# Batch 0's score pieces regrouped: the first three key blocks together by halves of the queries, the later ones in twos

## The chip, the cores and the metric

One core of a Trainium2 chip. The metric is the device time of one execution in microseconds (us), as a median of repeated runs; a profile gives in addition the span of one execution, which here is about 2 us shorter than its time.

## The reference

Grouped attention followed by a feed-forward layer with a squared ReLU, in float32:

```python
# q: 8 x 16 x 384 x 64, k and v: 8 x 4 x 384 x 64 (each kv head serves 4 query heads)
scores = (1 / 8) * q @ k^T ;  attn = softmax(scores) ;  o = attn @ v
x = o as 3072 x 1024
out = (max(x @ w_in, 0) ** 2) @ w_out        # w_in 1024 x 2048, w_out 2048 x 1024
```

## The kernel before

The kernel records all operations with their dependencies and an assumed duration, in a Python loop that at each step chooses what TensorE does next; the recorded order is then fixed for each engine. A *unit* is one block of 128 keys of one kv head, 12 in a batch; its scores have 2 x 768 columns. A *piece* is a part of them that goes through one pair of PSUM banks, `2 * (u % 2)` (u is here the piece's number), and one exponential on ACT:

```python
    def burst_small(b, pieces, base):
        n, c0, wide = (b * NU + pieces[0][0]) % NEX, pieces[0][1], pieces[0][2]
        ...                                     # scores: two matmuls (row halves) per unit in it, L341
        src = ps[:, base:base + 2, 0:total].rearrange("p x (k c) -> p x k c", k=len(pieces))
        dst = expT[:, n:n + len(pieces), :, c0:c0 + wide].rearrange("p k x c -> p x k c")
        R.add("scalar", lambda e: e.activation(dst, src, AF.Exp, scale=0.125), ...)     # L351

    for group in ((0, 1), (2, 3), (4, 5), (6, 7), (8, 9), (10, 11)):
        if 0 < group[0] < NU - 2:
            smalls += [[(u, 0, 512)] for u in group] + [[(u, 512, 256) for u in group]]
        else:
            smalls += [[(u, c0, 384)] for c0 in (0, 384) for u in group]
```

For batch 0 the rest of the head is, on TensorE: transposes of keys (L298) and queries (L315), attention times v in halves of 18 matmuls (L367; a half needs three units of its kv group), transposes of the result (L400), and the first four up-projection tiles (L425, 32 matmuls). Between these stand the transposes that batch 1 needs. The recorder lets the latter in by

```python
        if turn_q and (b == 0 or pairs < 6 or x_done[0] == 8) and (...):     # b: batch of the transpose
```

so after the sixth attention half they wait until all eight are transposed. After the head comes "the stretch": batch 1's scores and the other 12 up-projection tiles of batch 0 in fours (L462). Its first four need the third and fourth of eight blocks of w_in. The loads stand in POOL's queue in a fixed order, here its middle:

```python
    load_w_in(1)
    load_v(1)
    dup_k(1)
    for i in range(2, 6):
        load_w_in(i)
    aug_v(1, "gpsimd")            # waits for v of batch 1
    for i in range(6, 8):
        load_w_in(i)
```

The softmax here doesn't subtract the row's maximum and nothing guards it: scores larger than these inputs give would overflow.

## Time and profile before

| | |
|---|---|
| median, range of 3 runs | 419.39 us, 419.33 to 420.1 |
| span of the profiled execution | 1110.1 us |
| exponentials of batch 0 | 8 of 768 elements, 12 of 1024 |
| w_in, w_out | 8 blocks of 512 KB, 4 of 1024 KB |

The profile shows an execution 2.65 times as long as the timed ones.

### The profile page before, as it was taken

What the parts mean: (1) busy time and instruction counts of PE and PEld (TensorE: products, weight loads), DVE (VectorE), ACT (ScalarE), POOL (GpSimd) and SP (SyncE); (2) the same over time, 40 slices, a digit from 0 to 9 for tenths busy, and PEclk for the clock granted to TensorE, in tenths of its full rate; (3) what the DMA queues carried; (4) which work ended last, traced back from release to release, by engine and by line L of the source; (5) the groups of instructions that cost most, each with busy time, mean ns of one, the idle gap of its engine ahead of it and who ended that gap; (6) DMA issues with size and microseconds to landing.
All of it is one profiled execution on the core that took longest, in us unless ns stands there. A gap on an engine that the chain in (4) does not pass through costs nothing.

```text
span 1110.1 us, 9624 instructions
## 1 busy us (share of the span) xinstructions
PE 1107.0 (100%) x4330; PEld 446.8 (40%) x4330; DVE 203.8 (18%) x434; ACT 169.6 (15%) x181; POOL 48.0 (4%) x63
## 2 busy tenths in 40 slices
PE   9999999999999999999999999999999999999999
PEld 5544523454233532345323363243632336234323
DVE  3312201131011310114001141012300123001100
ACT  5233000330023100230003300032000320001100
POOL 7100101000100010000100000000000000000000
DMA  9950626102600070000700013000110001000000
GB/s 186 203 72 1 99 53 90 15 1 49 106 16 1 9 125 29 10 1 15 119 28 10 1 22 69 29 10 0 24 34 29 1 1 29 29 28 1 0 28 29
DMA packets 96921, 44.40 MB, mean 40 GB/s; under 512 B 77296, under 2 KB 90864, under 8 KB 96880
## 3 DMA queue, kind: packets, MB, share of 16 engines
q0 software_dynamic: 36544, 17.44, 12.2%
q1 hardware_dynamic: 59664, 25.86, 9.6%
q8 instruction: 34, 0.56, 0.2%
q10 hardware_dynamic: 672, 0.49, 0.1%
q14 instruction: 7, 0.06, 0.0%
HBM read 35.65 MB, written 12.58 MB: 43 GB/s over the span
## 4 chain that ended last, share of the span: by engine, by line
PE 100%; DVE 0%; issue 0%
PE ps L524 41%; PE ps L462 35%; PE ps L367 8%; PE ps L341 8%; PE ps L425 6%; PE ps L588 1%; PE ps L315 0%; PE ps L298 0%; PE ps L400 0%; DVE y_sb L533 0%
## 5 line engine op out<-in xcount | busy, mean ns | idle before, releaser
L524 PE MATMUL ps<-w_out_sb,h2T 128*128 128x512 bf16 (+2 forms) x784 | 460.1, 823 | 0.0
L462 PE MATMUL ps<-xT,w_in_sb 64*128 64x384 bf16 x1728 | 415.1, 681 | 0.0
L524 PEld LDWEIGHTS ps<-w_out_sb,h2T 128*128 128x128 bf16 x784 | 135.6, 175 | 309.0 <-issue 308.8
L462 PEld LDWEIGHTS ps<-xT,w_in_sb 64*128 64x128 bf16 x1728 | 153.7, 170 | 232.1 <-issue 221.8
L351 ACT ACTIVATE expT<-ps 128x1024 bf16<-128x1024 f32 (+1 forms) x146 | 146.8, 1012 | 583.7 <-PE ps L341 583.6
L475 DVE TENSOR_SCALAR hr<-ps 128x384 f32<-128x384 f32 x108 | 55.2, 553 | 371.5 <-PE ps L462 371.5
L341 PE MATMUL ps<-qT,kT 64*128 64x256 bf16 (+2 forms) x384 | 114.0, 651 | 0.0
L533 DVE COPY y_sb<-ps 128x512 f32<-128x512 f32 (+2 forms) x49 | 33.4, 681 | 406.5 <-PE ps L524 406.5
L367 PEld LDWEIGHTS ps<-v_aug,expT 128*128 128x128 bf16 x1152 | 87.1, 141 | 16.5 <-issue 12.9
L367 PE MATMUL ps<-v_aug,expT 128*128 128x65 bf16 x1152 | 90.8, 281 | 0.0
L425 PE MATMUL ps<-xT,w_in_sb 128*128 128x384 bf16 x160 | 73.1, 684 | 0.0
L341 PEld LDWEIGHTS ps<-qT,kT 64*128 64x128 bf16 x384 | 29.6, 150 | 54.5 <-issue 33.7
L482 DVE TENSOR_TENSOR h2T<-hr 128x384 bf16<-128x384 f32 x102 | 50.0, 551 | 0.0
L425 PEld LDWEIGHTS ps<-xT,w_in_sb 128*128 128x128 bf16 x160 | 27.4, 173 | 41.1 <-issue 41.0
L382 DVE TENSOR_TENSOR o_sb<-ps,rinv 128x384 bf16<-128x384 f32 x64 | 35.7, 557 | 2.2
L435 ACT ACTIVATE h2T<-hr 128x384 bf16<-128x384 f32 x20 | 10.5, 523 | 137.2 <-DVE hr L433 137.2
L479 ACT ACTIVATE h2T<-hr 128x384 bf16<-128x384 f32 x6 | 3.1, 523 | 158.9 <-DVE hr L475 158.9
L275 POOL COPY v_aug<-v_st 128x768 bf16<-128x768 bf16 x8 | 6.6, 830 | 460.0 <-PE ps L367 415.2
L376 DVE RECIPROCAL rinv<-ps 128x6 f32<-128x6 f32 x64 | 12.4, 194 | 51.1 <-PE ps L367 51.1
L433 DVE TENSOR_SCALAR hr<-ps 128x384 f32<-128x384 f32 x20 | 11.2, 558 | 54.5 <-PE ps L425 54.5
L241 POOL DMA_DIRECT2D q_st<-in_q_dram x17 | 14.8, 881 | 0.9 <-POOLq L829 0.8
L209 POOL DMA_DIRECT2D k_st<-in_k_dram x7 | 5.3, 755 | 156.2 <-DMA qT<-q_st 156.2
(29 smaller groups left out, 79.3 us busy)
## 6 DMA issues: line engine op xcount, KB each, us to landing
out_dram<-y_sb SPq DMA_DIRECT2D x47, 256.0 KB, 2.0
q_st<-in_q_dram POOLq DMA_DIRECT2D x14, 384.0 KB, 7.5
w_in_sb<-in_moe_w_in_dram POOLq DMA_DIRECT2D x8, 512.0 KB, 14.3
w_out_sb<-in_moe_w_out_dram POOLq DMA_DIRECT2D x4, 1024.0 KB, 27.6
v_st<-in_v_dram POOLq DMA_DIRECT2D x8, 192.0 KB, 8.4
k_st<-in_k_dram POOLq DMA_DIRECT2D x7, 192.0 KB, 3.8
q_st<-in_q_dram POOLq DMA_DIRECT2D x3, 192.0 KB, 5.4
xT<-o_sb SPq DMA_TRANSPOSE x28, 2.7
```

The source lines that it names most:

```text
L241: i = R.add("gpsimd", lambda g: g.dma_start(q_st[st][:, h0:h1, :], q[b, h0:h1].rearrange("h (p j) d -> p h (j d)", j=NJ)), writes=[("q_st" ...
L341: mm = pe.matmul(ps[:, base + x, m * wide:(m + 1) * wide], kT[b % 2][64 * x:64 * x + 64, u, :], q_cols(b, u // NJ, x, c0, c0 + wide))
L351: R.add("scalar", lambda e: e.activation(dst, src, AF.Exp, scale=0.125), reads=keys, writes=[("expT", (b * NU + u) % NEX, t) for u, _, _ i ...
L367: m = pe.matmul(po[:, f - 6 * s2, 0:D + 1], w, v_aug[b % 2][:, g * NJ + j, 0:D + 1], start=(j == 0), stop=(j == NJ - 1))
L376: R.add("vector", lambda e: e.reciprocal(rinv[r].ap().unsqueeze(2), po[:, :, D:D + 1]), reads=[("bank", i)], writes=[("rinv", r)], cost=0.22)
L382: R.add("vector", lambda e: e.tensor_tensor(dst, srcv, rbv, ALU.mult), reads=[("bank", i), ("rinv", r)], writes=[("o_sb", o, s2)], cost=0.48)
L425: m = pe.matmul(bank(i)[:, 0:S], w_in_sb[:, kc, c * 128:(c + 1) * 128], xT[b % NXT][:, kc, :], start=(kc == 0), stop=(kc == NKC - 1))
L462: m = pe.matmul(bank(4 + xs[x])[:, 0:S], w_in_sb[r, kc, c * 128:(c + 1) * 128], xT[b % NXT][r, kc, :], start=(phase < 2 and kc == 0), stop ...
L475: R.add("vector", lambda e, r=r, i=i: e.tensor_scalar_max(hr[r][:, :], bank(4 + i)[:, 0:S], 0.0), reads=[("bank", 4 + i)], writes=[("hr", ...
L482: hr_read[r] = (R.add("vector", lambda e, c=c, r=r: e.tensor_tensor(h2T[:, c, :], hr[r][:, :], hr[r][:, :], ALU.mult), reads=[("hr", r)], ...
L524: m = pe.matmul(bank(i)[:, 0:n], h2T[:, c, i3 * 128:(i3 + 1) * 128], w_out_sb[:, c, c0:c1], start=(c == 0), stop=(c == NFC - 1))
L533: R.add("vector", lambda e: e.tensor_copy(ysl, bank(i)[:, 0:n]), reads=[("bank", i)], writes=[("y", yb)], cost=0.08 + n / 960)
```

## The change

Its intent: ACT should have three pieces to do, not two, before it needs the second half of the first queries, and the first kv group should be complete earlier.

```diff
-    for group in ((0, 1), (2, 3), (4, 5), (6, 7), (8, 9), (10, 11)):
-        if 0 < group[0] < NU - 2:
+    for group in ((0, 1, 2), (3, 4), (5, 6), (7, 8), (9, 10), (11,)):
+        if len(group) == 2:
```

## The prediction

> **What bounds the kernel now.** I read the head of the page first, because its span does not fit the times. The medians of the timed runs are 419.39 us (419.33 to 420.1), the profiled execution took 1110.1. Next the chain that ended last in order of time, for the pace of the matmuls:
>
> ```profile
> span 1110.1 us, 9624 instructions
> PE 1107.0 (100%) x4330; PEld 446.8 (40%) x4330; DVE 203.8 (18%) x434; ACT 169.6 (15%) x181; POOL 48.0 (4%) x63
> ...
> 46.53 8.47 PE ps L425 x19
> 55.00 1.24 PE ps L341 x4
> 56.24 5.32 PE ps L462 x24
> ...
> 122.08 54.81 PE ps L524 x92
> 176.88 14.22 PE ps L462 x64
> ```
>
> The columns of the last five are start, length, engine, tile, line and count. 54.81 us for 92 matmuls of 512 columns is 596 ns each, 8.47 us for 19 of 384 columns is 446 ns, both 0.86 columns per ns, though the granted clock is listed as 1.000. So the execution I can look into ran TensorE at a pace that the timed runs can't have had: 2.65 times the time. In it TensorE is busy all the time and everything else hides behind it; the waits of TensorE in the first batch can't be read off it. ACT, DVE and transfer durations should not depend on that, and I use them.
>
> To find the head in the timed runs I rescale. At a full pace of N/2.4 + 2.5 ns (see below) 512 columns are 215.8 ns and 384 are 162.5, so the factors are 596/215.8 = 2.76 and 446/162.5 = 2.74; for 65 columns 76.6 ns (8.27 us for 108 in the chain) against 29.6, 2.59. After 55.00 us, where the scores of the second batch start, the chain holds some 457 us of line 524, 386 of 462, 60 of 425, 77 of 367 and 78 of 341. Rescaled: 166 + 141 + 22 + 30 + 28 = 387 us (estimate). That leaves 419.4 - 387 = 32 to 33 us for the head, with a microsecond or two of tail in it. TensorE's own work in the head is about 50.5 us of the slow trace (4.47 to 55.00), 18.4 us at full pace, and it begins at about 4.5. So TensorE should idle some 9 us in the head of a timed run. The head is what this change touches, and it is bound there by something other than TensorE.
>
> The candidate is the row of exponentials on ACT, with what feeds it:
>
> ```profile
> L351 ACT ACTIVATE expT<-ps 128x1024 bf16<-128x1024 f32 x138 | 140.4, 1024 | 577.5 <-PE ps L341 577.4
> L351 ACT ACTIVATE expT<-ps 128x768 bf16<-128x768 f32 x8 | 6.4, 810 | 6.2 <-PE ps L341 6.2
> ...
> 7.16 1.51 ACT L351 ACTIVATE expT<-ps 128x768 bf16<-128x768 f32 x2 [2.19 <-PE ps L341]
> 8.02 0.36 DVE L322 COPY qT<-ps 128x384 bf16<-128x384 bf16 x1 [1.56 <-PE ps L315]
> 8.31 0.83 POOL L275 COPY v_aug<-v_st 128x768 bf16<-128x768 bf16 x1
> 9.31 0.81 ACT L351 ACTIVATE expT<-ps 128x768 bf16<-128x768 f32 x1 [0.65 <-PE ps L341]
> 10.75 0.81 ACT L351 ACTIVATE expT<-ps 128x768 bf16<-128x768 f32 x1 [0.62 <-PE ps L341]
> ```
>
> In the timeline ACT does two exponentials, then stands for 0.65 us, does one, stands for 0.62. Its second pair needs the second half of the first kv group's queries, which only reaches qT with the DVE copy at 8.02 to 8.38. That is the gap the change aims at. Two exponentials of 768 back to back took 1.51 us, two of 1024 took 1.94 (timeline at 11.79). Batch 0 has 8 of the former and 12 of the latter: 4 x 1.51 + 6 x 1.94 = 17.7 us if never held up. In the slow trace they take 18.55 us within 30.3 (7.16 to 37.5), so ACT waits 11.8 us among them.
>
> **What the skill says.** "TensorE: Matmul & The Clock Gate", section "Back-to-back issue gap": N/2.4 + 2.5 ns warm; this trace shows 596 ns where that gives 215.8, so it does not agree, and I take the formula for the timed runs only because 387 + 32 fits 419. "ScalarE: Activation LUTs", section "What ACT_TABLE_LOAD costs": an ACTIVATE with immediates takes 186 + 0.833 N ns, and neighbours overlap by about 93. That gives 826 ns at 768 and 1039 at 1024; the rows show 810 and 1024, and the pair 1.51 = 2 x 0.81 - 0.11. It agrees.
>
> **The change, part by part.** It changes the list of score pieces of batch 0 alone. Before: units 0 and 1 by halves of 384 queries, units 2 to 9 in pairs as 512, 512, 2 x 256, units 10 and 11 by halves. After: units 0, 1, 2 by halves (six pieces of 384), pairs (3,4), (5,6), (7,8), (9,10), and unit 11 by halves (two). Both are 8 x 768 and 12 x 1024 elements: **ACT work 0, TensorE score columns 0, DVE work 0.** The built orders of instructions agree: SP and POOL are the same, and TensorE differs only up to the first tiles of the stretch in which batch 1 is scored. Three things move.
>
> (a) The third piece becomes (unit 2, first half), which needs no second half of the queries. What this gains is ACT's gap at full pace, not the 0.65 us of the slow trace. By hand: first keys cast at 3.70, transposed and copied (0.36) by about 4.65; first queries cast at 4.20, transposed, copied by about 5.15; scores 0.15 later, 0.35 long; first exponential at about 5.7, second to 7.15. The second half of the queries is cast at 4.97 whatever the pace, its transposes follow the two score pieces at about 5.75, its copy ends near 6.5, just as the first pair of banks comes free, and its scores are there at about 6.9 to 7.0. So at full pace ACT stands for 0 to 0.3 us. Gain 0 to 0.3, taken as 0.15.
>
> (b) Group 0 of the kv heads is complete after six pieces of 384 (4.5 us of ACT) instead of 4 x 0.755 + 3 x 1.02 = 6.1, and its first half after three (2.3, then v_aug at 9.14 us holds it) instead of five (4.0). So TensorE gets attention work 1.5 us earlier, while it is idle anyway, and less piles up later. Counting pieces, the eight attention halves become ready at 3.4, 4.5, 8.6, 10.7, 12.7, 13.7, 17.5, 18.3 us of ACT time against 4.0, 6.1, 8.1, 9.1, 13.2, 15.3, 16.8, 18.3. The first two halves stand as nine and nine matmuls around a score piece (one later half did before), so those scores wait up to 0.3 us less. ACT's room to lose is about 32 - 5.7 - 17.7 - 6 (end work, next) = 2 to 3 us over the head; I guess that a fifth of it goes. Gain 0 to 1.0, taken as 0.5.
>
> (c) The end. The last exponential is followed by the last attention half. Its group's first half becomes ready one piece later than before (17.5 against 16.8). And 12 transposes of batch 1's keys and queries, which stood inside the head (rows of lines 298 and 315 between score pieces), move behind the last transposes of o: 24 stand there now, 12 before. TensorE after the last exponential: before 18 attention matmuls (0.6), 26 up-projections x 0.1625 (4.2), 18 transposes x 0.056 (1.0) = 5.8; after 0.6 + 23 x 0.1625 (3.7) + 30 x 0.056 (1.7) = 6.0. Cost 0.2. DVE has six copies there in place of three to four (0.36 or 0.56 each), beside 17 up-projections (2.8 us), so they are mostly hidden; 0.1 for it.
>
> Sum: -0.15 - 0.5 + 0.2 + 0.1 = -0.35 us. Everything after is the same program, TensorE-bound, and only shifts. 419.39 - 0.35 = about 419.0.
>
> **Rivals.** One: transfers set the pace and swallow any shift. For it: they run at 184 to 207 GB/s in each 5 us window from 5 to 60 us; w_in's last two blocks land at 37.6 and 40.2 us (22.5 + 15.1, 23.3 + 16.9), the w_out blocks at about 45 to 62, the queries of batch 2 at about 65. Against it: in rescaled time the stretch begins near 32, wants those w_in blocks near 43, w_out's second half near 65, and scores of batch 2 stand behind 64 matmuls put there as filler (176.88 above). If it holds: 419.4. Two: the halted ACT is real, the gap is as large as in the slow trace or larger (a cold TensorE in the first microseconds doubles its transposes), and the filled attention takes away most ACT waits: -1.5 us, 417.9. For it: 2 to 3 us are missing in my account of the head. Against it: TensorE is in order, and the transposes of groups 1 and 2 wait for their query transfers (landing at 6.7 and 8.9) in both orders. Three: the end work grows by more than 0.3, because the transposes and their copies now come between the last xT chunk and the second batch, and its first scores also follow 8 quad matmuls: +0.8 us, 420.2.
>
> **Range and chances.** The known spread of three runs is 0.8 us; the parts can err by about 0.7 together. Predicted 419.0 us, range 418.0 to 420.0. Two per cent is 8.4 us, as much as all of TensorE's idle time in the head, and no work is added: faster by over 2% 0.01, within 2% 0.98, slower 0.01.
>
> **What would show it.** In the changed profile: 8 exponentials of 768 and 12 of 1024 in batch 0; ACT's third exponential following the second without a gap; attention matmuls before the first piece of 2 x 256; 24 transposes together ahead of the last 17 up-projections; from there on the same groups and durations. If that profile runs at full pace, the first score of batch 1 should stand at about 32 us, and ACT's waits among the twenty exponentials should sum to 2 or 3. In a slow one again, the span should move by under 1 us, since the sum of TensorE work is the same but for a few warm-up matmuls. The prediction is wrong if the head's end moves by over 1 us either way, if TensorE turns out to wait for w_in or batch 2's queries, or if the pace of TensorE itself differs between the kernels.

## The result, and the profile after

Ratios here and below are the mean time of one kernel's fast runs over that of the other's in the same rounds, so not quite the ratio of the medians quoted.

| | before | changed | ratio, 95% interval |
|---|---|---|---|
| with the prediction | 420.10 (5 runs) | 419.83 (5) | 1.0002, 0.9987 to 1.0017 |
| repeated (a2) | 419.54 (9 runs) | 419.53 (5) | 0.9999, 0.9987 to 1.0012 |

No gain shows. The times alone cannot exclude 0.35 us either, since its ratio, 0.9992, lies in both intervals. That 419.83 lies in the range is no credit to the reasons: no change at all lies in it too. The profiles decide, and in them the reasons given for the gain fail.

The changed kernel's page begins:

```profile
span 418.2 us, 9601 instructions
```

Its timeline on ACT, in the first 30 us (start, length, engine, line, what, count, idle before and its releaser):

```profile
5.79 16.81 ACT L351 ACTIVATE expT<-ps 128x768 bf16<-128x768 f32 x20 [0.76 <-PE ps L341]
```

All twenty exponentials of batch 0 stand without a gap, from 5.79 to 22.60. That looks like success; only the same view of the kernel before at full pace can tell. It is the first experiment.

### The profile page after: what moved, and what is told of

It reads as the page before. It is cut to its first block, busy times and chain, and to the rows that moved or that the text cites. A ratio compares the mean times of both kernels' runs of the same rounds, so it can differ in the third digit from the quotient of the medians.

```text
span 418.2 us, 9601 instructions
## 1 busy us (share of the span) xinstructions
PE 413.4 (99%) x4308; PEld 236.2 (56%) x4331; DVE 198.6 (47%) x434; ACT 159.0 (38%) x181; POOL 48.0 (11%) x63
## 4 chain that ended last, share of the span: by engine, by line
PE 97%; ACT 2%; issue 0%; DVE 0%
PE ps L524 39%; PE ps L462 34%; PE ps L367 8%; PE ps L341 7%; PE ps L425 6%; ACT expT L351 2%; PE ps L588 1%; PE ps L400 0%; PE ps L298 0%; PE ps L315 0%; DVE y_sb L533 0%
## 5 line engine op out<-in xcount | busy, mean ns | idle before, releaser
L524 PE MATMUL ps<-w_out_sb,h2T 128*128 128x512 bf16 (+2 forms) x761 | 165.7, 375 | 1.2
L462 PE MATMUL ps<-xT,w_in_sb 64*128 64x384 bf16 x1728 | 160.3, 323 | 0.0
L524 PEld LDWEIGHTS ps<-w_out_sb,h2T 128*128 128x128 bf16 x784 | 75.2, 98 | 86.6
L462 PEld LDWEIGHTS ps<-xT,w_in_sb 64*128 64x128 bf16 x1728 | 83.1, 94 | 57.8 <-DVE hr L475 2.1
L341 PE MATMUL ps<-qT,kT 64*128 64x512 bf16 (+2 forms) x384 | 54.3, 326 | 0.3 <-ACT expT L351 0.3
L367 PEld LDWEIGHTS ps<-v_aug,expT 128*128 128x128 bf16 x1152 | 37.0, 97 | 5.7 <-issue 1.1
L367 PE MATMUL ps<-v_aug,expT 128*128 128x65 bf16 x1152 | 39.1, 193 | 0.2 <-issue 0.2
L425 PE MATMUL ps<-xT,w_in_sb 128*128 128x384 bf16 x160 | 27.7, 326 | 0.0
L341 PEld LDWEIGHTS ps<-qT,kT 64*128 64x128 bf16 x384 | 17.8, 94 | 15.6 <-issue 2.1
L425 PEld LDWEIGHTS ps<-xT,w_in_sb 128*128 128x128 bf16 x160 | 15.4, 98 | 9.7 <-DVE xT L406 0.2
```

The source lines that it names most:

```text
L341: mm = pe.matmul(ps[:, base + x, m * wide:(m + 1) * wide], kT[b % 2][64 * x:64 * x + 64, u, :], q_cols(b, u // NJ, x, c0, c0 + wide))
L367: m = pe.matmul(po[:, f - 6 * s2, 0:D + 1], w, v_aug[b % 2][:, g * NJ + j, 0:D + 1], start=(j == 0), stop=(j == NJ - 1))
L425: m = pe.matmul(bank(i)[:, 0:S], w_in_sb[:, kc, c * 128:(c + 1) * 128], xT[b % NXT][:, kc, :], start=(kc == 0), stop=(kc == NKC - 1))
L462: m = pe.matmul(bank(4 + xs[x])[:, 0:S], w_in_sb[r, kc, c * 128:(c + 1) * 128], xT[b % NXT][r, kc, :], start=(phase < 2 and kc == 0), stop ...
L524: m = pe.matmul(bank(i)[:, 0:n], h2T[:, c, i3 * 128:(i3 + 1) * 128], w_out_sb[:, c, c0:c1], start=(c == 0), stop=(c == NFC - 1))
```

## The experiments

**a1: the kernel before, unchanged.**

> The kernel before, unchanged, for a profile at full TensorE pace (the first one ran at a third of it) and as a control of the noise. Ratio 1.000 within 0.002. Theory A (the exponentials of batch 0 already stand without a gap at full pace, so the change had nothing to win): the twenty exponentials take 16.8 to 17.3 us from 5.8, as in the changed kernel, and batch 1's first scores stand at 29.3 to 29.8 us. Theory B (the change did win in the head and lost it again): the exponentials here take 17.5 to 19 us, with gaps, and batch 1's first scores stand 0.5 us or more later than the changed kernel's 29.58, or the stretch after them is shorter.

Ratio 1.0002 (0.9987 to 1.0018), and a profile, span 418.2. Its timeline on ACT, then on TensorE further on:

```profile
5.77 16.91 ACT L351 ACTIVATE expT<-ps 128x768 bf16<-128x768 f32 x20
...
28.65 0.60 PE L341 MATMUL ps<-qT,kT 64*128 64x512 bf16 x4
29.09 1.46 PE L462 MATMUL ps<-xT,w_in_sb 64*128 64x384 bf16 x16
...
31.04 0.83 PE L462 MATMUL ps<-xT,w_in_sb 64*128 64x384 bf16 x8 [0.48 <-DMA w_in_sb<-in_moe_w_in_dram]
```

The kernel before has no gap in this row either: 16.91 us against 16.81, and 16.80 in e2 further down, which has the same order. This is theory A; B's 17.5 to 19 us fail. The gaps of 0.65 and 0.62 us in the slow profile came with its slow TensorE. They are absent although in this execution the second half of the queries was cast later (5.17 us) than in the changed kernel's profile (4.52).

My 29.3 to 29.8 us for batch 1's scores missed, because the two orders put them in different places: directly behind the up-projections here, after 8 matmuls of L462 in the changed kernel (29.47 there). The comparable mark is the end of the 32 up-projections, called **the head's end** from here on. (The chain's starts lie 0.07 to 0.17 us behind the timeline's here, so times are compared within one view.) The last line shows something new: TensorE waits for a w_in block, and in this execution the chain of what ended last runs through that transfer.

```profile
15.11 1.47 POOL k_dup L270
16.57 0.81 POOL w_in_sb L252
17.39 13.52 DMA w_in_sb<-in_moe_w_in_dram
```

It also shows why the block is late: in POOL's queue the copy of batch 1's keys (`dup_k(1)`) stands before this load, and here it had to wait for these keys until 15.11 us.

**a2: the changed kernel, unchanged.**

> The changed kernel, unchanged, 5 rounds more on the same chip as the control. Both theories: ratio 0.998 to 1.002; if the prediction's 0.35 us were there, 0.9992. The profile repeats: twenty exponentials from 5.8 to 22.6 without a gap, first scores of batch 1 at about 29.6, a wait of TensorE for w_in of about 0.4 us near 30.7.

Ratio 0.9999. The row and the scores repeat; the wait for w_in does not: in the first profile of this kernel the block landed at 30.66, its weights went in at 30.71, 0.37 us late, and the matmuls lost 0.16; here it landed at 29.83, in time. In a1 it was 30.91; in f1, shown further down, 29.69. So this landing moves by over a microsecond between executions, and it follows the issue: POOL issued the load at 17.39 us in a1, and at 15.66 in f1, where the keys had landed 1.7 us sooner.

From here I had two suspects: the row of exponentials as the bound of the head, with nothing won in it, and the w_in landing as a pin that hides what is won. e1 to e4 take the last of ACT's work away, take the pin away, or both. In e1 to e4 TensorE's order is unchanged to the last instruction.

**e1: ACT's last two exponentials cut short.** They do 16 of 384 queries, and DVE sets the rest to 1.0 at the start. Wrong, though it passed the comparison: with these inputs (0.1 times a normal draw) the exponentials are near 1.

```diff
+        w = 16 if b == 0 and pieces in smalls[-2:] else wide
-        src = ps[:, base:base + 2, 0:total].rearrange(...)
+        src = ps[:, base:base + 2, 0:total].rearrange(...)[:, :, :, 0:w]
-        dst = expT[:, n:n + len(pieces), :, c0:c0 + wide].rearrange(...)
+        dst = expT[:, n:n + len(pieces), :, c0:c0 + w].rearrange(...)
```

> Kernel before, but the last two exponentials of batch 0 do 16 of 384 queries (wrong result on purpose), TensorE's order untouched: ACT's row ends about 1.1 us sooner, near 21.6 us. Theory P (the arrival of w_in's fourth block near 30.8 us pins the stretch, so nothing won in the head is kept): batch 1's first scores move from 28.65 to 27.6-28.0, TensorE's wait for w_in grows from 0.5 to 1.2-1.6 us, total 0.0 to -0.2 us (ratio 0.9995 to 1.000). Rival R (the head's end sets the time, the change merely won nothing there): total -0.7 to -1.1 us (ratio 0.9974 to 0.9983).

Ratio 1.0001 (0.9988 to 1.0015). ACT's timeline, then the chain:

```profile
5.72 15.41 ACT L351 ACTIVATE expT<-ps 128x768 bf16<-128x768 f32 x19 [0.47 <-PE ps L341]
21.59 0.20 ACT L351 ACTIVATE expT<-ps 128x32 bf16<-128x32 f32 x1 [0.46 <-PE ps L341]
...
28.49 0.54 PE ps L341 x4
```

ACT is done at 21.79 in place of 22.68 in a1 and 22.55 in e2, and the head still ends at 28.49; e2, with all exponentials, has 28.60. These 0.11 us are not the cut's: the chains of the two profiles are apart by 0.11 already at the fifth score piece (8.69 and 8.80 us), long before it. So 0.8 to 0.9 us less at the end of ACT's row is worth nothing. The total is what theory P said, but its stage is wrong: the scores come no earlier for the cut, and there is no longer wait for w_in. Both theories assumed that the end of ACT's row bounds the head's end, and that falls: the last short exponential even waits for its scores. What a faster ACT in the whole row would do was not tested.

**e2: the pin loosened.** Batch 1's v load is moved behind w_in's sixth block (and its copy behind the eighth), after the orders were made, so that all compute engines but POOL have the old order.

```diff
+    MOVES = [("v1", "w5"), ("aug1", "w7")]     # operation, and the one it is put behind, before emit()
```

> Kernel before, only batch 1's v load moved behind w_in's sixth block and its copy behind the eighth, so w_in's blocks 3 to 6 land some 2 us sooner. Theory P: the wait for w_in near 31 us is gone, total -0.4 to -0.6 us (ratio 0.9986 to 0.999). Rival R: that wait is covered elsewhere, total 0.0 (0.9995 to 1.0005). Batch 1's scores stay at 28.65 in both.

Ratio 0.9996 (0.9983 to 1.0009), medians 419.31 against 419.40. The wait for w_in is gone and the span of the profile is 417.4. The timing cannot tell the 0.1 to 0.2 us from nothing, and 0.4 was expected; it compares with a mixture of executions in which the block comes in time and in which it doesn't.

**e3: e1 and e2 together.**

> e1 and e2 together (wrong result on purpose). Theory P: the shorter head is now kept, total -1.1 to -1.6 us (ratio 0.9962 to 0.9974), more than e1 and e2 added. Rival R: as e1, -0.7 to -1.1 us. If both fail (0.0), something later than w_in pins the time (w_out, or batch 2's queries).

Ratio 1.0001 (0.9989 to 1.0013), head's end 28.67, e2 28.60. Missed by both theories, and it follows from e1: the shorter ACT row gives TensorE nothing. A later pin, the third case, isn't needed to explain it, as the head's end did not move.

**e4: the changed kernel with e2's move.**

> The changed kernel with the same move of the v load as e2. Theory P plus equal heads: as e2 within 0.2 us, since without the pin the two orders' heads end at 28.65 and 28.82 plus 0.05: the changed one 0.0 to 0.2 us slower than e2 (ratio to the kernel before 0.9988 to 0.9994). Rival R2 (the pin hid a real gain of the change): 0.3 us or more faster than e2.

Ratio 1.0002 (0.999 to 1.0014), median 419.56, so 0.25 above e2; the spans are 417.7 and 417.4. So there is no sign of a hidden gain, R2's 0.3 us; the 0.25 lies just above the expected 0 to 0.2, and the forecast ratio, 0.9988 to 0.9994, was missed. With the pin gone in both, the two orders can be compared in the chain. First e2, then e4, from the last attention half to the head's end:

```profile
22.81 0.55 PE ps L367 x18
23.36 0.33 PE ps L425 x2
23.68 0.18 PE ps L400 x3
23.86 0.81 PE ps L425 x5
24.68 0.17 PE ps L400 x3
24.84 0.34 PE ps L315 x6
25.18 0.34 PE ps L298 x6
25.51 3.09 PE ps L425 x19
```

```profile
22.85 0.55 PE ps L367 x18
23.40 0.33 PE ps L425 x2
23.72 0.19 PE ps L400 x3
23.91 0.65 PE ps L425 x4
24.56 0.17 PE ps L400 x3
24.73 0.17 PE ps L298 x3
24.90 0.34 PE ps L315 x6
25.23 0.17 PE ps L298 x3
25.40 0.34 PE ps L315 x6
25.73 0.34 PE ps L298 x6
26.07 2.76 PE ps L425 x17
```

The last attention half starts at 22.81 and 22.85: all that the change does in the head up to there makes no difference. From there it takes 5.79 us to the head's end in one and 5.98 in the other: 24 transposes for 12, and 23 up-projections for 26. At 56 and 162.5 ns each that makes 0.67 - 0.49 = 0.18 us more. It repeats: by the starts in the timeline this part takes 5.89 us in all four profiles of the old order (a1, e1, e2, e3) and 6.07 to 6.08 in the three of the new one (changed kernel, a2, e4). In the stretch it becomes 0.3 us (end at 48.21 and 48.51).

What bounds the part before? The next experiments, for which I had to give up the ACT row as the bound, take work from TensorE alone.

**f1: lighter up-projections.** 24 of the head's 32 stream 96 columns in place of 384; wrong result (relative error 0.15).

```diff
+                    w = S if b or kc == 0 or kc == NKC - 1 else 96
-                    m = pe.matmul(bank(i)[:, 0:S], ..., xT[b % NXT][:, kc, :], ...)
+                    m = pe.matmul(bank(i)[:, 0:w], ..., xT[b % NXT][:, kc, 0:w], ...)
```

> Kernel before, but 24 of the 32 up-projection matmuls of the head stream 96 columns in place of 384 (wrong result on purpose); ACT, DVE and all orders as before. Theory Q (from about 10 us on TensorE's own work is the head's bound) with P (w_in's fourth block pins the stretch near 30-31 us): TensorE reaches batch 1's scores 1.6 to 2.6 us sooner (26.0 to 27.0), then waits 1.5 to 2.5 us for w_in, total 0.0 to -0.4 us. Rival R (ACT or the DVE chain bounds the head): batch 1's scores move by less than 0.6 us. Rival without pin: total -1.6 us or more.

Its timeline on ACT, then on TensorE:

```profile
5.38 16.73 ACT L351 ACTIVATE expT<-ps 128x768 bf16<-128x768 f32 x20 [0.39 <-PE ps L341]
...
27.27 0.61 PE L341 MATMUL ps<-qT,kT 64*128 64x512 bf16 x4 [0.17 <-DVE hr L433]
27.72 1.46 PE L462 MATMUL ps<-xT,w_in_sb 64*128 64x384 bf16 x16
29.82 0.83 PE L462 MATMUL ps<-xT,w_in_sb 64*128 64x384 bf16 x8 [0.64 <-DMA w_in_sb<-in_moe_w_in_dram]
```

Batch 1's scores come 1.38 us sooner than in a1, but only part of this is the edit's. ACT's row is about as long as ever (16.73 us), yet it ends at 22.11 in place of 22.68, above all because it starts 0.39 us sooner, 10 us before the first light matmul: in this execution TensorE's first transposes took 0.22 us each, in a1 mostly 0.31. Most of these 0.57 us is the execution's, not the edit's: in f2, with the same edit, the row ends at 22.54. From the start of the last attention half to batch 1's scores f1 takes 5.08 us, a1 5.89, and f2 below 5.09: the light matmuls are worth 0.8. So TensorE's own work behind the last exponential does hold a part of the head's end, in the direction of theory Q. But 0.8 lies between Q's 1.6 to 2.6 and R's 0.6, and both are missed: four copies on DVE at the tiles' ends now stand in the way, as the releaser in TensorE's first line shows. Before that, lighter work gains nothing: the last attention half still starts 0.08 us behind the last exponential, as in a1.

The fourth block of w_in lands at 29.69, and TensorE stands for 0.64 us: the total is 419.31 against 419.40 in the medians. The ratio, 1.0017, contains one run of 423.21 and says nothing.

**f2: f1 with e2's move.**

> f1 with batch 1's v load moved behind w_in's sixth block (as e2). Q and P: most of what f1 lost to the wait comes through, total -0.8 to -1.8 us (ratio 0.9957 to 0.998); remaining waits for w_in's sixth block or w_out may take the rest. Rival (the pin is not w_in): as f1, within 0.3 us.

Ratio 0.9988 (0.9976 to 1.0001), 0.5 us and not quite clear of nothing, with the same wrong result. Less than expected. What TensorE waits for between 20 and 82 us (us in total, times, longest):

```profile
PEld ps L524 <- DMA w_out_sb<-in_moe_w_out_dram: 0.8, 1, 0.8
PEld ps L341 <- DMA qT<-q_st: 0.8, 1, 0.8
```

So behind w_in's blocks stand two more transfers, w_out's and the transposed queries of batch 2. The scores of batch 2 start at 78.93 us, where e2 has them at 78.58, although the stretch ended at 47.38 in place of 48.21. The 0.5 us in the times are therefore not explained by this one profile (its execution, 419.68 us, was the slowest of five).

**h6: v_aug earlier, with e2's move, in the changed kernel.** If the first attention half is ready after three pieces and only v_aug and the transposes stand in its way, an earlier copy should let TensorE use its idle time.

```diff
-    dup_k(0, 3, 4)
-    aug_v(0, "gpsimd")
+    aug_v(0, "gpsimd")
+    dup_k(0, 3, 4)
```

> Changed kernel, with v_aug of batch 0 copied on POOL one copy earlier, so that the recorded order puts the first attention half (18 matmuls) ahead of the last two groups' transposes, in TensorE's idle time near 9.5 us, and with e2's move of the v load. Theory (the change's early readiness was blocked by v_aug and the transposes): the head's up-projections end 0.3 to 0.6 us before e4's 28.83, at 28.2 to 28.5; total -0.3 to -0.8 us against the kernel before. Rival (TensorE fills up anyway and its first idle time is bound by the exponentials): end at 28.7 to 28.9, total -0.2 to +0.2 us.

Slower: ratio 1.0031 (1.0018 to 1.0044), head's end 29.18, which neither expected. The recorder now puts the 18 matmuls ahead of the sixth score piece, and v_aug is there only at 8.70 us. ACT's timeline:

```profile
5.55 3.67 ACT L351 ACTIVATE expT<-ps 128x768 bf16<-128x768 f32 x5 [0.49 <-PE ps L341]
9.85 13.28 ACT L351 ACTIVATE expT<-ps 128x768 bf16<-128x768 f32 x15 [0.63 <-PE ps L341]
```

Here is a real gap of 0.63 us in the row, its end moves from 22.6 to 23.13, and the head's end by 0.35. This does not show what a longer ACT row alone costs, since TensorE itself stood for v_aug and was late with the scores. How the two engines stand to each other is seen from e3 and f2: by the timeline less work on ACT does not bring the last attention half forward (22.71 us in e3, 22.64 in e2), nor does less on TensorE (22.62 in f2), as both come to it at about the same time. The time lost in all, 1.2 us against e4's median, is more than these 0.35, and the span's 0.8 contains a pause of 0.28 us at 54 us for which no wait is shown; the rest was not followed up.

**e8: 9 of the moved transposes allowed back into the head, with e2's move, in the changed kernel.**

```diff
-        if turn_q and (b == 0 or pairs < 6 or x_done[0] == 8) and (...):
+        if turn_q and (b == 0 or pairs < 8 or x_done[0] == 8) and (...):
```

> Changed kernel, with 9 of batch 1's 12 moved transposes allowed back into the head (condition pairs < 6 made pairs < 8) and with e2's move of the v load. Theory Q: where they stand within TensorE's busy part does not matter, up-projections end at 28.75 to 28.9 as in e4 (28.83). Rival (the moved transposes are the cost, the prediction's step c): 28.5 to 28.65, as in e2 (28.60).

The chain, to the head's end:

```profile
5.74 8.00 ACT expT L351 x10
...
22.14 1.11 PE ps L367 x36
...
24.73 0.17 PE ps L298 x3
24.89 0.34 PE ps L315 x6
25.23 0.34 PE ps L298 x6
25.56 3.09 PE ps L425 x19
```

Head's end 28.65, where e4 has 28.83 and e2 28.60; the stretch ends at 48.26 (48.51, 48.21). The number is the rival's, but by luck. Until the sixth attention half the order is e4's, and already its tenth exponential ends at 13.74 us where e4's ends at 13.89 (7.99 + 5.90 in its chain); by the timeline the last attention half starts at 22.53 against 22.69. This lead of the execution is nearly all of the 0.18. From there to the head's end e8 takes 6.05 us, e4 6.08 and e2 5.89. Nine transposes (0.50 us) left the end, and three up-projections (0.49) took their place, so e8 gains nothing there, and it cannot single out the transposes. It does confirm the count: three transposes more than in e2 make 0.17 us, and 0.16 were measured. (The time, ratio 1.001 with 0.9997 to 1.0023, is not better: that profile has a pause of 0.62 us near 53 us, see the last section.)

## Why the prediction was wrong

- **What bounds the head.** Half right. It said that the head is "bound there by something other than TensorE", namely ACT's row, with 2 to 3 us of room in it. In the changed kernel's chain ACT's row leads from 5.79 to 13.87 us; the rest is TensorE:

```profile
5.79 8.08 ACT expT L351 x10
```

  In the kernel before, ACT leads in the chain of e2 for only 3.00 us. The room is what was not there: the twenty exponentials stand without waits in both orders, 16.8 to 16.9 us, where 2 or 3 us of waits were forecast. (The forecast's 17.7 us of work counts the overlap of 0.11 us within pairs only, not between them.) And TensorE comes to the last attention half at about the same time as ACT, as e3 and f2 show. The room came from subtracting: the head was put at 32 to 33 us by rescaling the slow trace, and it ends at 28.6. That "387 + 32 fits 419" was no check, as the 32 is 419.4 - 387. The time also contains some 2 us outside the span, which I had not taken off, and the rest of the error lies in a remainder of two large numbers.
- **Step a, ACT's gap, taken as 0.15.** The hand calculation was good: first exponential at 5.7 (measured 5.77), gap 0 to 0.3 (none in a1, a2, e2 and the changed kernel). In e4, where the queries of the next group landed at 7.04, the changed order itself has a gap of 0.21 us after its third piece.
- **Step b, attention work that is ready earlier, taken as 0.5.** This is the step that carried the gain, and it failed: the last attention half starts at 22.81 and 22.85. The 2 to 3 us of room, of which it was to be a fifth, were not there, and TensorE did not get attention work earlier. By the timeline the first two halves, forecast 1.5 us earlier, start at 10.94 and 11.91 us in e4, at 11.05 and 12.03 in e2. What they need is there sooner (v_aug at 9.10 in a2); they stand behind other work in TensorE's order. The third and fourth start later, at 14.25 and 16.15 against 13.71 and 14.68, as the prediction's own list has it (8.6 and 10.7 us of ACT time against 8.1 and 9.1). That the later third and fourth are what cancels the gain was not tested by itself.
- **Step c, the end, cost 0.2 plus 0.1.** Right: 5.8 against 6.0 us from the last attention half were predicted for TensorE, 5.79 against 5.98 measured, and the difference repeats in seven profiles. What costs is the sum of what stands there; e8 does not tie it to the moved transposes alone. The 0.1 for DVE did not appear in the head; the 0.3 at the stretch's end is near the sum.
- **Rival one, transfers swallow any shift.** I gave it 419.4 and argued that the stretch begins near 32 us, late enough for w_in. It begins at 28.6, and a wait for w_in, which the prediction names among its signs of being wrong, came in a1 and in the changed kernel's first profile. By the timeline the kernel before comes to the fourth block at 28.98 + 1.30 = 30.28 us (e2), the changed one at 29.90 + 0.65 = 30.55 (a2). When it lands later than both (30.91 in a1, 30.66 in the changed kernel), both go on when it is there and the 0.3 us are hidden; when it lands earlier (29.83 in a2, 30.02 in e1), the changed kernel is later by them. Of the 1.4 us that f1 is ahead in the head, its median keeps 0.1, behind the wait for w_in; f2's profile loses its 0.8 to w_out and batch 2's queries, though its times keep some 0.5.

So the expected gain did not exist, since ACT's row was already full and the attention halves that TensorE was to do earlier did not start earlier; the order pays 0.2 us at the head's end and 0.3 at the stretch's, and a late transfer can hide this. What stays open: the size of the net effect, since the times of both comparisons allow anything from -0.5 to +0.7 us, and what the halves of step b would be worth in another order. No version here beats both kernels: e2 is the best one that keeps the result, at 0.9996 not distinguishable from before.

## What to carry to other kernels

A gap in a profile taken at another pace than the timed runs is not a gap to be closed: compare the span with the times first, and get the kernel before once more at full pace before reading waits from it. Where an engine's row is full, ask of the chain which engine the last piece of it waits for; here taking 0.9 us off ACT's row gave nothing, as TensorE came to the same point at the same time, which a share of busy time can't tell. Before an earlier end is put down to an edit, look whether the profile was already ahead before the edited part, as in e1, f1 and e8. And before work is moved inside a start-up phase, look at which transfer the next phase needs first: a phase that ends 1.4 us sooner in front of a load that lands at 29.7 us has won little.

## What the Trainium skill lacked or had wrong

- "TensorE: Matmul & The Clock Gate", section "Back-to-back issue gap": it gives N/2.4 + 2.5 for an isolated matmul and says that it over-counts at large N. Here it holds for streams at full pace. From 374.33 us the changed kernel's chain has 128 matmuls of 384 columns in 20.80 us, 162.5 ns each, as it gives; e2 has 92 of 512 columns in 19.86 us, 215.9 against 215.8. The sustained 131 ns for 512 columns that the same section states was not seen.
- The same page, section "What's actually happening", knows 1.2 and 2.4 GHz. The slow profile streamed 512 columns in 596 ns, 0.86 per ns, with a listed clock of 1.000. Neither state explains it, nor do the stuck quarter clock and the limit of 13/16 that the page mentions further on, and no run here shows the cause.
- No page says how far a load's landing moves between executions of one program: the same w_in block was there at 30.91, 30.66 and 29.69 us (a1, changed kernel, f1, all with the same order of loads).
- No page that I found explains a pause of TensorE, 0.21 to 0.62 us at 53 to 54 us, before the last attention matmuls of batch 1, with no wait shown. It is in 4 of 11 fast profiles (changed kernel, e3, h6, e8) and not in the other seven. A fetch of 16 KB of instructions starts between 50 and 52.1 us in profiles with it (51.5 in the changed kernel) and without it (51.1 in a2), so this does not settle it; its cause is open.
